# First stage of an attention, FFN and experts kernel: turned tokens, weight pieces and x's place

## The chip, the cores and the metric

One core of one Trainium2 chip. The metric is the device time of one execution in microseconds; lower is better. The engines are called TensorE (PE in rows; PEld is its weight load), VectorE (DVE), ScalarE (ACT), GpSimd (POOL) and SyncE (SP).

## The reference, cut to what matters

```python
# attention, for each of B=4 batches and H=8 heads; x: 512 x 64 tokens, state: 32 x 64 slots
scores = scale * x @ state.T                # 512 x 32
a = softmax(scores);   xread = a @ state    # softmax over the 32 slots
scores2 = scale * state @ x.T               # 32 x 512
a2 = softmax(scores2); sread = a2 @ x       # softmax over the 512 tokens
y = concat([xread, sread]), heads side by side   # 4 x 544 rows of 512
# FFN: y = g @ w_out with h = y @ w_in, g = h - tanh(h)    (512 -> 2048 -> 512)
# experts: gates from 8 normalisation rounds, sum over 8 experts of relu(y @ w1[e]) @ w2[e]
```

The FFN's weights arrive as 64-bit numbers and are taken apart in the kernel; fp32 products are made from a first part (hi, fp32r) and a second (lo) of each operand, in three matmuls (`mm3`, L92 to L95).

## The kernel before, in words

Three stages follow one another. **The first stage** is the attention of all four batches together with round 0 of the FFN. **Rounds 1 to 7** of the FFN follow (a round is 256 of the 2048 inner columns). **The expert stage** fills the rest.

In the first stage a batch b has four pairs p of heads and two groups q of two pairs. The steps, with the letters by which the order names them:

- x (`load_x`, L229): batches 0 and 1 head by head, 2 and 3 by token tile, into tiles [token, t, head, d] of their own (two buffers). A token's number is 4p + t for partition p.
- T (`tokens`, L285): four transposes turn a pair's 512 tokens into [2 x 64, 512]; t copies the result to SBUF (`keep_tokens`).
- S (`scores`, L294): two fp32 matmuls, slots as weights (128x64), the turned tokens as moving operand: scores with slots on partitions. m and 5 take the largest per row, c (`keep_scores`) copies the scores to SBUF, X is the exponential with its sum (softmax over tokens).
- O (`over_slots`, L312): four transposes of the kept scores give half of the token tiles with tokens on partitions; o, 6, E, R, 1, 2, N make the softmax over slots (o, 6, R, 1, 2 on VectorE, E on ScalarE, N on either VectorE or GpSimd).
- B (`back`, L367): four transposes of the exponentials; b copies them. G (`read`, L393): eight fp32 matmuls, the exponentials as weights (128x64), 128 columns of x moving; g (`keep_read`, L406) scales 32x64 blocks by the inverse sums (3, 4) into rows. J, Q, i (`xs_turn` and its two parts, L415 to L426) turn all rows of sread at the end.
- W, w, l: the slots' weights turned and split for the FFN's first product. M, k, r (`m_mul`, `m_hi`, `m_lo`): state times w_in, split. H, a, s, z, q: h, tanh, gate and its split (q is `h_lo` on GpSimd). Y, y: the second FFN product and its copy to the result tiles `yacc[b]`.
- F, A, I, j, C, K: the conversion of a weight piece of 128 x 256: fetch, two ScalarE steps (`words_of`), three VectorE steps (`bits_of`, L158 to L171), one GpSimd step (`number_of`), the first part by ScalarE (`hi_of`) and the second by GpSimd (`lo_of`). The first stage converts 16 pieces, for rounds 0 and 1.

`ORDER_OF_FIRST` (L737) is a list of such words, like T10 or b10V (step, batch, number, engine A, V or G). `listed` (L690) pins each word behind the last instruction of every engine, so within a word list every queue has the order of the list. What follows the list (rounds 1 to 7, and the conversion of pieces by `prep`, L198) isn't pinned: a scheduler lays it out, and it may stand between the words of the list. In the rounds `prep` runs one step of conversion per call, with fetches two pieces ahead (`AHEAD`).

`sb_turn` (L251) turns the state into block form; the state comes in through `yacc[3]`. PSUM has four banks `bank` (tag w) and four `acc_bank` (tag a); before, only the FFN's second product uses the latter in this stage.

Of the kernel before, what the change touches and what calls it, by code (L numbers as in the profile page):

```python
# [19 lines left out]
def attention_ffn_experts(  # L20
# [31 lines left out]
    AHEAD = 2  # L52
# [53 lines left out]
    if True:  # L106
# [20 lines left out]
        for j in range(NJ):  # L127
            for k in range(KD):
                pieces.append(("i", j, k, 0, w_in[k * P:(k + 1) * P, j * FC:(j + 1) * FC]))
            for f in range(2 * j, 2 * j + 2):  # L130
                for c in range(0, DM, FC):
                    pieces.append(("o", j, f, c, w_out[f * P:(f + 1) * P, c:c + FC]))

        late = pieces[2 * KD + 2:3 * KD]
        pieces[2 * KD + 2:4 * KD] = pieces[3 * KD:4 * KD] + late
        live = {}
        FIRST_PIECES = 4 * KD
        at = [FIRST_PIECES]

        def piece(step):  # L140
            return step if FIRST_PIECES <= step < len(pieces) else -1

        def fetch(n):
            if n < len(pieces) and n not in live:
                raw = mid.tile([P, FC, 2], U32, tag="raw", bufs=AHEAD + 3, name=f"raw{n}")
                nc.sync.dma_start(raw.rearrange("p n w -> p (n w)"), pieces[n][-1].bitcast(U32))
                live[n] = {"raw": raw}

        def temp(n, tag, dtype, bufs):
            live[n][tag] = mid.tile([P, FC], dtype, tag=tag, bufs=bufs, name=f"{tag}{n}")  # L150
            return live[n][tag]

        def words_of(n):
            v = live[n]
            nc.scalar.activation(temp(n, "mag", F32, 2), f32(v["raw"][:, :, 1]), AF.Abs, scale=REBASE)
            nc.scalar.mul(temp(n, "low", U32, 3), v["raw"][:, :, 0], 2.0 ** -29)

        def bits_of(n):  # L158
            v = live[n]
            t = temp(n, "bits", U32, 4)  # L160
# [16 lines left out]
        def hi_of(n):  # L177
            v = live[n]
            kind, j, r, c, _ = pieces[n]
            if kind == "i":  # L180
                hi = ffn.tile([P, FC], F32R, tag="wih", bufs=6, name=f"wih{j}_{r}")
                lo = ffn.tile([P, FC], F32R, tag="wil", bufs=6, name=f"wil{j}_{r}")
                wi_t[j, r] = hi, lo
            else:
                if r not in wo_t:
                    wo_t[r] = (
                        ffn.tile([P, DM], F32R, tag="woh", bufs=4, name=f"woh{r}"),
                        ffn.tile([P, DM], F32R, tag="wol", bufs=4, name=f"wol{r}"),
                    )
                hi, lo = (z[:, c:c + FC] for z in wo_t[r])  # L190
# [38 lines left out]
        def load_x(b, i):  # L229

            if b not in x_t:
                x_t[b] = att.tile([P, NT, H, D], F32, tag="x", bufs=2, name=f"x{b}")
            if b > 1:
                nc.sync.dma_start(x_t[b][:, i], x[b].rearrange("h (p t) d -> t p h d", t=NT)[i])
            else:
                nc.sync.dma_start(x_t[b][:, :, i], x[b, i].rearrange("(p t) d -> p t d", t=NT))
# [33 lines left out]
        sr = yacc_s  # L270
# [3 lines left out]
        class Attention:  # L274
# [3 lines left out]
            def __init__(self, b):  # L278
                self.b = b
                self.x = x_t[b].rearrange("p t h d -> p t (h d)")  # L280
                self.xt, self.sc, self.e2t, self.e1, self.ps = {}, {}, {}, {}, {}
                self.mx = att.tile([P, NQ], F32, tag="mx2", bufs=2, name=f"mx2_{b}")
                self.sm = att.tile([P, NQ], F32, tag="sm2", bufs=2, name=f"sm2_{b}")

            def tokens(self, p):  # L285
                ps = self.ps["t", p] = bank(f"xtps{self.b}_{p}")
                for t in range(NT):
                    nc.tensor.transpose(ps[:, t * P:(t + 1) * P], self.x[:, t, p * P:(p + 1) * P], ident)

            def keep_tokens(self, p, copy):  # L290
                self.xt[p] = att.tile([P, S], F32, tag="xt", bufs=4, name=f"xt{self.b}_{p}")
                copy(self.xt[p], self.ps.pop(("t", p)))

            def scores(self, q):  # L294
                b = self.b
                ps = self.ps["s", q] = bank(f"sc2ps{b}_{q}")
# [3 lines left out]

            def keep_scores(self, q):
# [1075 lines left out]
```

## Time and profile before

| | |
|---|---|
| median of 3 runs | 1775.64 us (1775.09 to 1775.74) |
| the profiled execution's own time | 1775.18 us |
| its span | 1773.4 us |
| TensorE busy | 1747.0 us, 99%, 8181 instructions |
| VectorE busy | 1201.2 us, 68% |
| ScalarE busy | 794.3 us, 45% |
| GpSimd busy | 1193.5 us, 67% |
| share of TensorE on the chain of waits | 86% |

The span runs from the first instruction to the last; the execution's own time is 1.8 us longer. Shares are of the whole span, so they say little about a stage of some 100 us: for that the busy time by stretches is to be read. A matmul's duration in a row is that of one instruction from end to end; since matmuls overlap, the time that one takes up is the distance of the starts.

### The profile page before, as it was taken

Reading aid. Unit: us, or ns where it says so; the run is one execution under the profiler, and the core shown is the slowest. Engines: PE = TensorE matmul, PEld = TensorE weight load, DVE = VectorE, ACT = ScalarE, POOL = GpSimd, SP = SyncE. Lnnn points to the kernel's source line nnn. Section 1 sums busy time; section 2 is a strip of 40 time slices with the busy share of each in tenths; the row PEclk is TensorE's granted clock in tenths of the full one; section 3 lists DMA queues with packets and bytes.
Section 4 is the critical chain, followed back from the end, with each engine's and each line's share of the span. In section 5 each row is a group of like instructions: output and inputs, shape, how many; then the busy total and the mean of one; then the engine's idle time right before and its main releaser. Section 6 shows DMA issues by size and latency. Waiting matters only on the chain.

```text
span 1773.4 us, 23139 instructions
## 1 busy us (share of the span) xinstructions
PE 1747.0 (99%) x8181; PEld 1441.1 (81%) x8181; DVE 1201.2 (68%) x1793; ACT 794.3 (45%) x1399; POOL 1193.5 (67%) x1041
## 2 busy tenths in 40 slices
PE   7999999999999999999999999999999999999998
PEld 5778888878888888888888888888888888888887
DVE  8998787556876566666666666756666666666666
ACT  7876666444333323323333323344444444444442
POOL 3575556278777677767666676567777777777774
PEclk9999999999999999999999999999999999999999
DMA  5221110017666556665556565455554655655541
GB/s 148 83 92 48 48 48 19 24 57 235 210 208 221 194 192 210 209 208 203 198 196 208 192 207 191 190 208 205 198 202 173 231 202 188 215 187 201 206 184 53
DMA packets 158759, 296.73 MB, mean 167 GB/s; under 512 B 28404, under 2 KB 107828, under 8 KB 154292
## 3 DMA queue, kind: packets, MB, share of 16 engines
q1 hardware_dynamic: 157604, 295.00, 48.3%
q8 instruction: 64, 1.05, 0.2%
q14 instruction: 51, 0.42, 0.1%
q10 hardware_dynamic: 1040, 0.26, 0.1%
HBM read 174.87 MB, written 120.36 MB: 166 GB/s over the span
## 4 chain that ended last, share of the span: by engine, by line
PE 86%; DVE 7%; ACT 3%; POOL 2%; issue 1%; DMA 1%; SPq 0%; DVEq 0%; ACTq 0%; POOLq 0%
PE p1b L1075 14%; PE p_P L1226 14%; PE p1a L1075 10%; PE p1c L1075 9%; PE p L95 7%; PE p L93 7%; PE p L94 7%; PE p1s L1127 2%; PE yps L94 2%; PE yps L93 2%; PE mP L1226 2%; PE yps L95 2%; DVE low L164 2%; PE hps L95 1%; DVE bits L168 1%
## 5 line engine op out<-in xcount | busy, mean ns | idle before, releaser
L868 POOL TENSOR_TENSOR w1l<-w1r,w1h 128x768 fp32r<-128x768 f32 (+1 forms) x96 | 170.9, 1806 | 156.9 <-ACT w1h L866 156.9
L1178 DVE SCALAR_TENSOR_TENSOR oacc<-p,pr,oacc 128x512 f32<-128x512 f32 x224 | 166.4, 745 | 111.9 <-PE p L95 111.9
L1075 PE MATMUL p1b<-xT,w1h 128*128 128x512 f32 x768 | 237.6, 390 | 0.0
L1235 DVE TENSOR_TENSOR m<-p_P,m 128x512 f32<-128x512 f32 x232 | 159.5, 689 | 86.3 <-PE p_P L1226 86.3
L93 PE MATMUL p<-w2b,hh 128*128 128x512 f32 x512 | 199.8, 390 | 1.8 <-ACT hh L1013 1.5
L94 PE MATMUL p<-w2b,hh 128*128 128x512 f32 x512 | 199.3, 389 | 0.0
L95 PE MATMUL p<-w2b,hl 128*128 128x512 f32 x512 | 197.0, 390 | 0.7 <-DVE hl L1014 0.7
L1083 DVE TENSOR_TENSOR U<-p1b,P 128x512 f32<-128x512 f32 x128 | 88.4, 691 | 150.5 <-PE p1b L1075 126.6
L1075 PEld LDWEIGHTS p1b<-xT,w1h 128*128 128x128 f32 x768 | 142.4, 188 | 28.1
L1075 PE MATMUL p1a<-xB,w1h 128*128 128x512 f32 x512 | 161.0, 395 | 0.0
L494 POOL TENSOR_TENSOR gl<-t,gh 128x512 fp32r<-128x512 f32 x64 | 86.5, 1362 | 107.9 <-ACT gh L490 106.8
L1075 PE MATMUL p1b<-xT,w1l 128*128 128x512 f32 x384 | 149.5, 389 | 0.0
L903 ACT CAST w2s<-w2r 128x1024 fp32r<-128x1024 f32 x32 | 33.7, 1052 | 231.3 <-POOL w2r L897 231.3
L1032 POOL TENSOR_TENSOR h11l<-U,h11h 128x512 fp32r<-128x512 f32 x32 | 41.4, 1295 | 126.7 <-ACT h11h L1031 67.3
L1233 ACT COPY m<-p_P 128x512 f32<-128x512 f32 x128 | 74.9, 586 | 98.2 <-PE p_P L1226 97.9
L1014 DVE SCALAR_TENSOR_TENSOR hl<-U,hh 128x512 fp32r<-128x512 f32 x64 | 99.2, 1550 | 27.8 <-ACT hh L1013 27.8
L93 PEld LDWEIGHTS p<-w2b,hh 128*128 128x128 f32 x512 | 96.1, 188 | 23.0 <-ACT hh L1013 2.6
L865 POOL TENSOR_TENSOR w1r<-w1r 128x256 f32<-128x256 f32 x128 | 94.3, 747 | 28.5 <-DMA w1r<-in_moe_w_dram 25.6
L95 PEld LDWEIGHTS p<-w2b,hl 128*128 128x128 f32 x512 | 96.0, 188 | 21.1 <-DVE hl L1014 1.3
L94 PEld LDWEIGHTS p<-w2b,hh 128*128 128x128 f32 x512 | 96.1, 188 | 19.7
L1083 DVE TENSOR_TENSOR U<-p1c,U 128x512 f32<-128x512 f32 x128 | 87.9, 686 | 33.3 <-PE p1c L1075 33.0
L1075 PEld LDWEIGHTS p1a<-xB,w1h 128*128 128x128 f32 x512 | 93.6, 188 | 17.9
(301 smaller groups left out, 4809.2 us busy)
## 6 DMA issues: line engine op xcount, KB each, us to landing
w1h<-w1h SPq DMA_DIRECT2D x64, 896.0 KB, 4.3
w1l<-w1l SPq DMA_DIRECT2D x64, 896.0 KB, 6.0
w<-w2a SPq DMA_DIRECT2D x30, 1024.0 KB, 4.8
w<-w2c SPq DMA_DIRECT2D x30, 768.0 KB, 8.2
w1r<-in_moe_w_dram SPq DMA_DIRECT2D x128, 128.0 KB, 4.4
w2r<-in_moe_w_dram SPq DMA_DIRECT2D x32, 512.0 KB, 4.0
w2a<-w2b SPq DMA_DIRECT2D x60, 256.0 KB, 3.2
w2c<-w2s SPq DMA_DIRECT2D x60, 256.0 KB, 3.8
```

Of the source, the lines that this page charges most:

```text
L93: nc.tensor.matmul(ps, whi, xhi, start=start, stop=False, **k)
L94: nc.tensor.matmul(ps, whi, xlo, start=False, stop=False, **k)
L95: nc.tensor.matmul(ps, wlo, xhi, start=False, stop=stop, **k)
L494: nc.gpsimd.tensor_tensor(out=lo, in0=h_t1.pop((j, b, i)), in1=f32(hi), op=ALU.subtract)
L865: nc.gpsimd.tensor_tensor(out=r[:, out], in0=r[:, a], in1=r[:, b], op=op)
L868: nc.gpsimd.tensor_tensor(out=lo[:, c0:c1], in0=r[:, c0:c1], in1=f32(hi[:, c0:c1]), op=ALU.subtract)
L1014: nc.vector.scalar_tensor_tensor(out=lo, in0=src, scalar=0.0, in1=f32(hi), op0=ALU.max, op1=ALU.subtract)
L1075: nc.tensor.matmul(t[z], w[:, slot, k, :], x[:, m, k, :], start=(first and k == i == 0), stop=(k == 1 and i == 2), skip_group_check=True,)
L1083: nc.vector.tensor_tensor(out=t[name], in0=a, in1=b, op=ALU.add)
L1178: nc.vector.scalar_tensor_tensor(out=o, in0=ps, scalar=w, in1=o, op0=ALU.mult, op1=ALU.add)
L1226: nc.tensor.matmul(ps, w[:, a], b, start=(i == 0 and not goes_on), stop=(i == 2 and (last or not kept)), skip_group_check=True,)
L1235: nc.vector.tensor_tensor(out=m, in0=ps, in1=m, op=ALU.add)
```

## The change

- **Tokens** are turned by plain matmuls against the identity, head by head (weights 128x64 of x, 128 moving columns), into `acc_bank`; `scores` goes there too.
- **Scores over slots** no longer come from kept scores: for each token tile and pair the turned tokens are weights (128x128) and the state's 64 columns move. `keep_scores` goes; the exponential reads the scores in PSUM. O, o, 6, E, R, 1, 2, N work by group q instead of by half.
- **The second softmax**: 3 and 4 (sums, inverses) work by q; D makes a diagonal of the inverse sums, and B multiplies the exponentials by it instead of transposing them. G has x as weights (128x64) and 32 columns of the turned exponentials as moving operand, so sread comes out turned; g and h split it batch by batch. `keep_read` and the step J, Q, i go.
- **Weight pieces** have 512 columns (two k blocks of w_in or a whole row block of w_out): 8 pieces in the first stage instead of 16; in the rounds a piece every second step, fetched one ahead. Conversion steps of the first pieces behind the list are pinned.
- **x** lies by head in the result tiles `yacc[b]`, loaded two heads at a time (16 loads instead of 24). Turned tokens of batches 0 and 1 lie in the tiles of the gate's split.
- **M**: four of eight second parts go to GpSimd, from a copy that ScalarE makes (n, rG). Shares: four of eight on VectorE (one before).
- 13 matmuls of the identity by itself stand ahead of the list, and the list is new.

The core of the diff:

```diff
-    AHEAD = 2
+    AHEAD = 1
...
+            for k in range(0, KD, 2):
+                of = w_in[k * P:(k + 2) * P, j * FC:(j + 1) * FC].rearrange("(k p) n -> p k n", p=P)
+                pieces.append(("i", j, k, of))
             for f in range(2 * j, 2 * j + 2):
+                pieces.append(("o", j, f, w_out[f * P:(f + 1) * P, :]))
...
         def piece(step):
-            return step if FIRST_PIECES <= step < len(pieces) else -1
+            n = step // 2
+            return n if step % 2 == 0 and FIRST_PIECES <= step and n < len(pieces) else -1
...
             if b not in x_t:
+                x_t[b] = yacc[b].rearrange("p k s -> p (k s)").rearrange("p (h t d) -> p h t d", h=H, t=NT)
+            nc.sync.dma_start(
+                x_t[b][:, 2 * i:2 * i + 2].rearrange("p h t d -> p h (t d)"),
+                x[b, 2 * i:2 * i + 2].rearrange("h (p t) d -> p h (t d)", t=NT),
+            )
...
             def tokens(self, p):
+                ps = self.ps["t", p] = acc_bank(f"xtps{self.b}_{p}")
                 for t in range(NT):
-                    nc.tensor.transpose(ps[:, t * P:(t + 1) * P], self.x[:, t, p * P:(p + 1) * P], ident)
+                    for r in range(2):
+                        nc.tensor.matmul(
+                            ps[D * r:D * (r + 1), t * P:(t + 1) * P], self.x[:, 2 * p + r, t, :], ident,
+                            start=True, stop=True,
+                        )
...
-                for q in range(NQ):
-                    for t in (2 * half, 2 * half + 1):
-                        o = (t % 2) * 256 + q * P
-                        nc.tensor.transpose(ps[:, o:o + P], self.sc[q][:, t * P:(t + 1) * P], ident)
+            def over_slots(self, q):
+                b = self.b
+                ps = self.ps["o", q] = bank(f"sc1ps{b}_{q}")
+                for t in range(NT):
+                    for p in (2 * q, 2 * q + 1):
+                        c = col0(b, p)
+                        nc.tensor.matmul(
+                            ps[:, t * P + c:t * P + c + 64], self.xt[p][:, t * P:(t + 1) * P],
+                            sb_raw[:, b // 2, p, c:c + 64], start=True, stop=True,
+                        )
...
+            def diagonal(self, q):
+                self.dg[q] = att.tile([P, P], F32, tag="dg", bufs=2, name=f"dg{self.b}_{q}")
+                nc.vector.tensor_scalar_mul(self.dg[q], ident, self.sm[:, q:q + 1])
...
-                    nc.tensor.transpose(ps[:, t * P:(t + 1) * P], self.sc[q][:, t * P:(t + 1) * P], ident)
+                    nc.tensor.matmul(
+                        ps[:, t * P:(t + 1) * P], self.sc[q][:, t * P:(t + 1) * P], self.dg[q], start=True, stop=True
+                    )
...
+            def read(self, _):
+                b = self.b
+                ps = self.ps["r"] = bank(f"srps{b}")
+                for p in range(NP):
+                    for t in range(NT):
+                        for r in range(2):
+                            o = t * P + col0(b, p) + NS * r
+                            nc.tensor.matmul(
+                                ps[D * r:D * (r + 1), p * NS:(p + 1) * NS], self.x[:, 2 * p + r, t, :],
+                                self.e2t[p // 2][:, o:o + NS], start=(t == 0), stop=(t == NT - 1),
+                            )
...
+        def m_keep(j, bp, q, copy):
+            m_raw[j, bp, q] = yacc_s if q else att.tile([P, 2 * FC], F32, tag="n", name=f"mraw{j}_{bp}")
+            copy(m_raw[j, bp, q], m_ps[j, bp, q])
...
-                prep()
+                listed(prep) if at[0] < PINNED else prep()
...
+        warm = acc_bank("warm")
+        for _ in range(13):
+            nc.tensor.matmul(warm[:, :P], ident, ident, start=True, stop=True)
```

The new list begins `x20 F01 x23 x22 T20 x11 x21 t20A U00 A01 F06 U10 u00 T23 u10 v10 T22` and ends, like the old one, with the last products Y of batch 3.

## Rows read from the trace of the kernel before

**Rows 1.** Busy time by stretches; columns: stretch, length, busy us (instructions) by engine, clock, DMA

```profile
0.00:40.00 40.00, 29.49 (x191) 21.65 (x191) 32.66 (x77) 29.95 (x66) 10.60 (x19) 0.96 0.59 152
40.00:104.00 64.00, 57.47 (x355) 43.43 (x355) 62.04 (x137) 53.30 (x127) 39.02 (x45) 1.00 0.29 91
104.00:385.00 281.00, 278.66 (x1330) 231.34 (x1329) 212.80 (x342) 173.66 (x364) 154.45 (x151) 1.00 0.12 38
```

**Rows 2.** TensorE's waits in 0 to 104 us, first, third and last of 16

```profile
PE xtps L288 <- DMA x<-in_x_dram: 5.8, 1, 5.8
...
PE srps L401 <- ACT e2t L374: 1.5, 1, 1.5
...
PE srps L401 <- DVE e2t L374: 0.2, 1, 0.2
```

**Rows 3.** TensorE's waits in 104 to 385 us, the two largest of three

```profile
PE ysps L95 <- DVE gsl L90: 1.2, 4, 0.3
PE yps L94 <- POOL gl L494: 0.6, 1, 0.6
```

**Rows 4.** Groups of VectorE's instructions in 0 to 104 us

```profile
L164 DVE SCALAR_TENSOR_TENSOR low<-raw,low 128x256 uint32<-128x256 uint32 x24 | 13.4, 565 | 0.3 <-ACT low L156 0.3
L450 DVE TENSOR_TENSOR ml<-mps,mh 64x512 fp32r<-64x512 f32 x16 | 11.0, 686 | 0.2
...
L413 DVE TENSOR_SCALAR yacc_s<-srps,sm 32x64 f32<-32x64 f32 x20 | 5.6, 281 | 0.3
...
L349 DVE TENSOR_SCALAR m<-m 128x16 f32<-128x16 f32 x8 | 2.2, 295 | 0.0
```

**Rows 5.** Groups of TensorE's instructions in 0 to 104 us

```profile
L288 PE MATMUL xtps<-ident,x 128*128 128x128 f32 x64 | 11.4, 329 | 6.2 <-DMA x<-in_x_dram 5.8 <-DVE mx L306 0.4
...
L401 PE MATMUL srps<-x,e2t 128*64 128x128 f32 x128 | 9.4, 281 | 1.6 <-ACT e2t L374 1.5 <-DVE e2t L374 0.2
```

**Rows 6.** TensorE in order of time, 51 to 54 us; columns: start, us, engine, line, operation

```profile
51.42 1.09 PE L401 MATMUL srps<-x,e2t 128*64 128x128 f32 x16
52.44 1.09 PE L288 MATMUL xtps<-ident,x 128*128 128x128 f32 x8
53.29 0.47 PE L93 MATMUL yps<-gh,woh 128*128 128x512 f32 x1
```

**Rows 7.** One line's instructions: shortest, median and longest in ns (L401, L656, L667)

```profile
L401 PE MATMUL srps<-x,e2t x128: 272/273/413, 18.6 to 69.4; 128*64 128x128 f32 x128
...
L656 PE MATMUL ltps<-add,lt x16: 251/251/272, 379.1 to 384.6; 16*128 16x8 f32 x16
...
L667 PE MATMUL lps<-x2s_raw,wg x8: 275/275/377, 392.6 to 393.5; 128*128 128x128 f32 x8
```

**Rows 8.** TensorE in order of time at 379 and at 392 us

```profile
379.08 1.05 PE L656 MATMUL ltps<-add,lt 16*128 16x8 f32 x8
...
392.62 1.16 PE L667 MATMUL lps<-x2s_raw,wg 128*128 128x128 f32 x8
```

**Rows 9.** Loads in 0 to 110 us: count, KB each, median us to landing

```profile
x<-in_x_dram SPq DMA_DIRECT2D x8, 256.0 KB, 3.7
```

**Rows 10.** TensorE in order of time, 5 to 11 and 34 to 37 us

```profile
5.81 1.09 PE L288 MATMUL xtps<-ident,x 128*128 128x128 f32 x4 [5.81 <-DMA x<-in_x_dram]
...
10.99 2.25 PE L299 MATMUL sc2ps<-xt,sb_raw 128*64 128x512 f32 x8
...
34.83 1.97 PE L288 MATMUL xtps<-ident,x 128*128 128x128 f32 x8
36.45 0.78 PE L93 MATMUL hps<-ath,mh 128*128 128x512 f32 x1
```

**Rows 11.** Busy time by stretches, 35 to 36 us (the clock is third from the end)

```profile
35.00:36.00 1.00, 1.00 (x6) 1.00 (x7) 0.96 (x3) 0.49 (x1) 0.00 (x0) 0.50 0.00 0
```

**Rows 12.** Groups of GpSimd's instructions in 0 to 104 us

```profile
L175 POOL TENSOR_TENSOR bits<-bits,low 128x256 uint32<-128x256 uint32 x22 | 16.8, 761 | 34.0 <-DVE bits L168 23.9 <-DVE sm L365 8.4 <-DVE low L164 1.2
L494 POOL TENSOR_TENSOR gl<-t,gh 128x512 fp32r<-128x512 f32 x8 | 10.7, 1342 | 3.2 <-ACT gh L490 3.2
```

More of the change, by code (lines that the diff above doesn't have):

```diff
@@ L269, in attention_ffn_experts @@
         at_t = {}
-        sr = yacc_s
         xs_hi = ffn.tile([P, KD, P], F32R, name="xs_hi")
@@ L326, in less_largest @@
                 v, m = self.ps.pop(("o", half))
-                e = att.tile(list(v.shape), F32, tag="e1", bufs=2, name=f"e1_{self.b}_{half}")
+                e = att.tile(list(v.shape), F32, tag="e1", bufs=4, name=f"e1_{self.b}_{half}")
                 nc.vector.tensor_tensor(
@@ L391, in weights_lo @@
                 nc.vector.tensor_tensor(out=lo, in0=self.ps.pop(("w", q)), in1=f32(hi), op=ALU.subtract)
-            def read(self, q):
+            def read(self, _):
                 b = self.b
-                ps = self.ps["r", q] = bank(f"srps{b}_{q}")
-                for t in range(NT):
-                    for g in range(2):
-                        u = 4 * q + 2 * ((g + b) % 2)
-                        nc.tensor.matmul(
-                            ps[64 * g:64 * (g + 1), :2 * D], self.e2t[q][:, t * P + 64 * g:t * P + 64 * (g + 1)],
-                            self.x[:, t, u * D:(u + 2) * D], start=(t == 0), stop=(t == NT - 1),
-                        )
@@ L415, in xs_turn @@
-        def xs_turn():
-            ps = h_ps["xs"] = bank("xsps")
-            for k in range(KD):
-                nc.tensor.transpose(ps[:, k * P:(k + 1) * P], sr[:, k * P:(k + 1) * P], ident)
-        def xs_hi_of():
-            nc.scalar.copy(xs_hi, h_ps["xs"].rearrange("a (k c) -> a k c", k=KD))
-        def xs_lo_of():
-            nc.vector.tensor_tensor(
-                out=xs_lo, in0=h_ps.pop("xs").rearrange("a (k c) -> a k c", k=KD), in1=f32(xs_hi), op=ALU.subtract
-            )
+                ps = self.ps["r"] = bank(f"srps{b}")
@@ L429, in m_mul, with read_lo @@
+            def read_lo(self, _):
+                hi, lo = (z[:, :, NS * self.b:NS * (self.b + 1)] for z in (xs_hi, xs_lo))
+                ps = self.ps.pop("r")[:, :KD * NS].rearrange("a (k s) -> a k s", k=KD)
+                nc.vector.tensor_tensor(out=lo, in0=ps, in1=f32(hi), op=ALU.subtract)
         def m_mul(j, bp, q):
@@ L446, in m_hi, with m_lo_kept @@
                 nc.scalar.copy(hi, v)
+        m_raw = {}
+        def m_keep(j, bp, q, copy):
+            m_raw[j, bp, q] = yacc_s if q else att.tile([P, 2 * FC], F32, tag="n", name=f"mraw{j}_{bp}")
+            copy(m_raw[j, bp, q], m_ps[j, bp, q])
+        def m_lo_kept(j, bp, q):
+            m_ps[j, bp, q] = m_raw.pop((j, bp, q))
+            for v, hi, lo in m_parts(j, bp, q):
+                nc.gpsimd.tensor_tensor(out=lo, in0=v, in1=f32(hi), op=ALU.subtract)
+            del m_ps[j, bp, q]
         def m_lo(j, bp, q):
@@ L723, in attention_ffn_experts @@
             PARTS[z] = lambda b, n, fn=fn: fn(b)
-        for z, fn in zip("Mkr", (m_mul, m_hi, m_lo)):
+        for z, copy in COPY.items():
+            PARTS["n" + z] = lambda b, n, copy=copy: m_keep(b // 2, b % 2, n, copy)
+        for z, fn in (("M", m_mul), ("k", m_hi), ("rV", m_lo), ("rG", m_lo_kept)):
             PARTS[z] = lambda b, n, fn=fn: fn(b // 2, b % 2, n)
```

136 lines of the change are left out of this document (59 added, 77 removed), and 4 rows, old and new, of the table PARTS.

## The prediction

> **What bounds the kernel now.** I read the busy time by stretches first, then TensorE's waits, then the instructions in order of time. The stretches show the parts [rows 1]: in 0 to 104 us, the first stage, VectorE is busy 94.7 us of 104 (32.66 + 62.04), and TensorE's row has holes; from 104 to 385 us TensorE is busy 278.66 us of 281, and behind that no less. So the span is TensorE's work plus its holes, and nearly all holes lie in the first stage. The waits give them [rows 2]: 5.8 us until the first piece of x, then 15 short waits of 0.2 to 1.5 us with 11.0 us in sum, most released by VectorE or ScalarE. From 104 to 385 us the waits are 1.8 us in the two largest groups [rows 3]. What VectorE does in the first stage is mostly small: the weight conversions, the second parts of M, the 32x64 scalings of the second read, and steps of 16 columns [rows 4].
>
> So VectorE holds TensorE up by some 11 us and not more; a change that relieves VectorE can earn those 11 us, and pays for each microsecond of matmul that it adds.
>
> **Prices on TensorE.** A plain fp32 matmul stands in the trace as two instructions, a transpose as one: the reads are 64 matmuls and x128, the turned tokens 64 transposes and x64 [rows 5]. Both kinds stand beside each other at full clock [rows 6]: 16 read instructions (weights 128x64, 128 moving columns) take 1.02 us from start to the next start, and within the block, whose last instruction takes 0.273 us from end to end [rows 7], (1.09 - 0.273) / 15 = 0.0545 us each; 8 transposes take 0.85 us, 0.106 each. With weights of 128 columns a short matmul is dearer [rows 7, 8]: eight with 8 moving columns take 1.05 us, (1.05 - 0.251) / 7 = 0.114 each, and eight with 128 moving columns (1.16 - 0.275) / 7 = 0.126. Eight columns cost as much as 128, so what limits them is the load, not the stream.
>
> **The change on TensorE, part by part.**
> Turned tokens (L288): 16 blocks of 4 transposes, 0.425 us each, become 16 blocks of 8 matmuls against the identity, 16 instructions of exactly the read's shape: 1.02 us. +9.5 us.
> Scores over slots (L317): 8 blocks of 4 transposes (0.42 us) become 8 blocks of 8 matmuls, 16 instructions with 128x128 weights and 64 moving columns. Nearest is 0.114: 1.82 us a block, +11.2 us. If the load hid wholly, 0.0545: +3.6.
> Turning back with the diagonal (L370): 4 transposes become 4 matmuls, 8 instructions of 128x128 by 128. At 0.126 that is 1.01 us against 0.42, eight times: +4.7 us. At 0.0545: +0.1.
> Second read (L401): 2 blocks of 1.02 us per batch become one of 32 matmuls, 64 instructions with 128x64 weights and 32 moving columns. No row has this shape. If only moving columns counted, a quarter of 0.0545, it would be 0.9 us a batch, -4.7 us in all; at the price of a 128-column load, 0.114, 7.3 us, +21. Weights of 64 columns stand at 0.0545, and moving columns hardly mattered where the load was the longer, so I take 0.0545: 3.5 us a batch, +5.8 us.
> The Trainium skill's page TensorE: Matmul & The Clock Gate, section LDWEIGHTS, states that a weight load takes its columns divided by 1.2 in ns, whatever the number of rows; its section on the 56 ns gap gives about 25 ns as the least distance of two short matmuls. By the first the read would be 53 ns an instruction, its term +5.5 us and the sum below +30.5, by the second 25 ns, -1.8 and +23.2, estimates from that page; no row here has 64-column weights with few moving columns, so the trace doesn't decide between them.
> The turn of the slots' rows (L418) goes: four transposes, -0.4 us.
> Sum: 9.5 + 11.2 + 4.7 + 5.8 - 0.4 = **+30.8 us** of TensorE work; low ends together +8.1, high ends +46.
>
> **What it takes back.** The first block of tokens needed four loads of x, issued one after the other from 0.74 us on; now it needs the first alone. A load of 256 KB, the new size, takes 3.7 us to landing [rows 9]; with 0.7 us for its issue (an estimate) TensorE starts near 4.4 instead of 5.81: -1.4 us.
> The first 24 transposes (4, 8 and 12) took 5.18 us, from 5.81 to 10.99, where 24 x 0.106 is 2.5, so they ran at half pace; from 34.83 us 8 transposes took 1.62 us instead of 0.85 [rows 10], with the granted clock at 0.50, the level of 1.2 GHz, after TensorE had waited for e2t [rows 2, 11]. Together 3.4 us. The 13 dummy matmuls (26 instructions) need nothing but the identity, so they run while x is on its way and cost nothing themselves; if they raise the clock, they take back up to 2.6 us. I take 2.5 of the 3.4.
> Of the 11.0 us of waits I take 8 back and leave 3, between none and all, for VectorE's relief.
>
> VectorE: the scalings in L413 go (5.6 us), half of the second parts of M (8 x 0.69 = 5.5) go to GpSimd; three more shares on VectorE cost perhaps 1 us each (estimate, above the 0.69 of another 512-column step), the diagonals and the sums by half perhaps 4 (estimate: some 20 instructions, most shorter than the 0.295 us of a 16-column step); weight pieces of 512 columns halve the count of three conversions, worth between nothing (if they cost by column) and half (if by instruction), which is 6.7 us for the largest of them; I take 3 for the three [rows 4]. Net some 7 us off 94.7, in a stage that becomes longer: VectorE is under 85% busy there and no longer the bound. GpSimd takes 8 halves of M at about 1.34, the price of its 512-column split [rows 12]: +10.7 against 49.6 busy [rows 1]; hidden under TensorE. ScalarE loses the eight copies of the scores and gains four of M. The first conversions for the round after the stage, which now stand in it as well (x24 where the stage needs 16), are pinned behind it, one more relief of VectorE. SP loses 8 loads of x and 8 of weights. x lying in the result tiles adds a wait of the first copy of y of each batch on its last read; in the order of the parts that read comes well before, so it costs nothing; were it late, ScalarE's later copies and the banks of y would queue behind it.
>
> From 104 us on nothing changes but the wide pieces, under a TensorE that is full there [rows 1]: 0. The expert stage is untouched.
>
> **The forecast.** 30.8 - 1.4 - 2.5 - 8 = +18.9 us. The profiled execution took 1775.18 us with a span of 1773.4; the median of the runs shown is 1775.64, so it stands for them. 1775.2 + 18.9 = **1794.1 us**. Its own range is 1780 (over slots, diagonal and read together 10 us cheaper, all waits and all of the clock back) to 1805 (of the three, only the earlier start comes back).
>
> **The rivals.**
> *Faster: the loads hide.* If short fp32 matmuls run as fast as their moving columns let them, TensorE's addition is near 8 us, less than the 1.4 + 3.4 + 11.0 = 15.8 us that can come back: 8 - 15.8 is -8, some 1767 us. It decides at an addition of 15.8. For it: VectorE is the fuller engine in the first stage now [rows 1]. Against it: eight moving columns at 0.114 [rows 8]. 13%.
> *No change.* The addition is 13 to 19 us, because over slots, diagonal and read run at half to two thirds of the prices I took, and all 15.8 us come back: 1772 to 1779. 10%.
> *Much slower: the clock falls.* The new over-slots and read blocks, 8 x 1.82 + 4 x 3.5 = 29 us, stream few columns a load; if half of that ran at 1.2 GHz, 14 us come on top: 1808. For it: the clock did fall once, at 35 us, after TensorE had stood still for 1.5 us [rows 2, 11]. The Trainium skill, same page, Part 1, says that "the default state is throttled, and activity releases the throttle"; this trace shows one such fall and no stretch of loads with 32 columns each. 8%.
> *Wide pieces late.* GpSimd's single instruction grows from 0.76 to about 1.34 us [rows 12] and stands ahead of gl, for which TensorE waits 0.6 us now [rows 3]; with 1 us in each of seven rounds +7, 1801. Inside the forecast's range.
>
> **How the numbers follow.** 0.2% of this kernel, about what a measurement can tell from no change, is 3.6 us. Faster 13%; same 10%; slower 77%, of which 69% is the forecast with the late pieces and 8% the clock. The range for 8 in 10 leaves out the faster case below and half of the clock case above, with a little of the case of no change: 1773 to 1808.
>
> **What would show it.** Right: in the first stage the tokens' x256 near 0.055 us from one to the next, over slots x128 near 0.11, the diagonal x64 near 0.12, the read x256 near 0.055; TensorE's row full from about 5 us on, VectorE's with gaps, the step to the even part (seen at 104 us now) near 120 us, and the expert stage as long as before. Wrong: over slots or the read well below these prices; or TensorE's holes as large as before, which would mean that another wait took VectorE's place; or a longer second part, which would point to the wide pieces.

## The result and the profile after

The changed kernel takes **1800.37 us** (median of four runs, 1800.2 to 1801.66), the one before, run beside it, 1775.55 (four runs): a ratio of **1.0142**, 95% interval 1.0124 to 1.0159. Slower, by 24.8 us where 18.9 were forecast. The profiled execution took 1800.44 us, its span is 1798.6, 25.2 more than before.

Busy time of the changed kernel by stretches, columns as in [rows 1]:

```profile
0.00:40.00 40.00, 32.77 (x312) 28.58 (x314) 26.37 (x49) 24.37 (x46) 16.99 (x19) 0.91 0.58 191
40.00:104.00 64.00, 64.00 (x655) 54.43 (x650) 45.72 (x105) 39.57 (x79) 28.94 (x23) 1.00 0.13 43
...
150.00:160.00 10.00, 6.74 (x37) 5.30 (x35) 9.19 (x12) 6.58 (x12) 7.23 (x6) 1.00 0.34 122
160.00:170.00 10.00, 6.71 (x26) 5.31 (x26) 9.82 (x15) 8.15 (x15) 6.88 (x5) 0.83 0.46 159
170.00:180.00 10.00, 5.80 (x19) 4.46 (x20) 9.89 (x13) 5.31 (x10) 8.58 (x6) 0.83 0.18 61
```

VectorE's first stage is lighter than forecast: 72.1 us busy of the first 104 instead of 94.7. Up to the first turn of the gated rows (`tsps`, at 116.5 us instead of 99.2) it is 78.5 us instead of 89.9, so 11.4 less where some 7 were forecast. TensorE is full from 40 to 150 us. But there is a hole before 40 us, and three lean stretches at 150 to 180 us, in round 1 and at its end, where VectorE is as full as it had been in the first stage.

TensorE's waits of the changed kernel, in 0 to 130 us (two rows, that is all there are) and in 130 to 411 us (the first three and the fifth of six); columns: line, releaser, sum in us, times, longest:

```profile
PE atps L398 <- DVE e L367: 5.6, 1, 5.6
PE warm L774 <- POOL ident masks.py:199: 1.5, 1, 1.5
...
PE hps L93 <- DVE gsl L90: 3.4, 1, 3.4
PE hps L95 <- DVE ml L467: 3.2, 1, 3.2
PE mps L93 <- DVE ml L467: 3.1, 1, 3.1
...
PE yps L94 <- POOL gl L511: 0.6, 1, 0.6
```

The fifteen short waits of [rows 2] have become one of 5.6 us. Three waits of over 3 us stand where [rows 3] showed nothing above 1.2.

TensorE's groups in 0 to 130 us, to be set beside [rows 5]:

```profile
L290 PE MATMUL xtps<-ident,yacc 128*64 128x128 f32 x256 | 16.7, 284 | 0.0
...
L323 PE MATMUL sc1ps<-sb_raw,xt 128*128 128x64 f32 x128 | 15.6, 276 | 0.0
...
L386 PE MATMUL e2ps<-dg,sc 128*128 128x128 f32 x64 | 9.5, 298 | 0.1
...
L419 PE MATMUL srps<-e2t,yacc 128*64 128x32 f32 x256 | 8.2, 223 | 0.0
```

What an instruction takes up is read in order of time, from start to next start. TensorE of the changed kernel at the start, around 27 us and from 40 to 48 us:

```profile
1.46 5.33 PE L774 MATMUL warm<-ident 128*128 128x128 f32 x26 [1.46 <-POOL ident masks.py:199]
6.72 1.09 PE L290 MATMUL xtps<-ident,yacc 128*64 128x128 f32 x16
7.75 1.09 PE L256 MATMUL sbps<-ident,yacc 128*128 128x128 f32 x8
8.77 3.71 PE L290 MATMUL xtps<-ident,yacc 128*64 128x128 f32 x64
...
27.07 1.09 PE L398 MATMUL atps<-ident,e 128*128 128x128 f32 x4 [5.63 <-DVE e L367]
28.29 2.05 PE L386 MATMUL e2ps<-dg,sc 128*128 128x128 f32 x8
29.99 0.56 PE L93 MATMUL mps<-wih,sb_hi 128*128 128x256 f32 x1
...
40.59 1.16 PE L386 MATMUL e2ps<-dg,sc 128*128 128x128 f32 x8
41.51 0.36 PE L93 MATMUL mps<-wih,sb_hi 128*128 128x256 f32 x1
...
42.30 1.89 PE L323 MATMUL sc1ps<-sb_raw,xt 128*128 128x64 f32 x16
44.13 1.09 PE L290 MATMUL xtps<-ident,yacc 128*64 128x128 f32 x16
45.05 1.03 PE L308 MATMUL sc2ps<-xt,sb_raw 128*64 128x512 f32 x4
45.91 2.01 PE L419 MATMUL srps<-e2t,yacc 128*64 128x32 f32 x64
47.75 1.06 PE L308 MATMUL sc2ps<-xt,sb_raw 128*64 128x512 f32 x4
```

A block of tokens takes 1.03 us (6.72 to 7.75), 0.0545 an instruction as forecast; a block over slots 1.83 (42.30 to 44.13), 0.114; the diagonal 0.92, 0.115. The read surprises: 64 instructions in 1.84 us, **0.029 each**, where I took 0.0545. And the dummies take 5.26 us, 0.2 each, so the first tokens start at 6.72 us, 0.9 later than in [rows 10].

These prices are means. How single instructions start is seen when the window is ended a little later each time. The read, in windows that end at 45.92, 45.95 and 46.01 us:

```profile
45.91 0.20 PE L419 MATMUL srps<-e2t,yacc 128*64 128x32 f32 x2
45.91 0.26 PE L419 MATMUL srps<-e2t,yacc 128*64 128x32 f32 x4
45.91 0.32 PE L419 MATMUL srps<-e2t,yacc 128*64 128x32 f32 x6
```

They start in pairs. The loop alternates between the two halves of the output's partitions, and an instruction for one half starts together with its neighbour for the other; the next pair follows 0.058 us later. So 0.029 is half the distance of two pairs. The tokens start in pairs too, 0.109 us apart with 128 moving columns, and so did the read before [rows 6]: their 0.0545 is half of that. Over slots, where each weight has all 128 columns, there are no pairs: one instruction starts every 0.112 us.

**The ledger.** I split both runs at two events: the second turn of a round's gated rows (`tsps`), at 111.07 us before and 125.02 after, and the one two rounds later, at 193.72 and 217.88. In each stretch an instruction is given the distance to the next start, less the wait that the profile names there:

| us | before | after | difference |
|---|---|---|---|
| turned tokens | 10.2 | 15.8 | +5.6 |
| over slots | 4.5 | 14.9 | +10.4 |
| turning back, diagonal | 4.2 | 8.1 | +3.9 |
| second read | 8.7 | 7.7 | -1.0 |
| turn of the slots' rows | 0.8 | 0 | -0.8 |
| dummies | 0 | 5.3 | +5.3 |
| all other matmuls | 66.1 | 66.2 | +0.1 |
| before the first instruction | 5.8 | 1.5 | -4.3 |
| waits | 10.8 | 5.6 | -5.2 |
| **to the first event** | 111.1 | 125.0 | **+14.0** |
| next two rounds, waits | 0.3 | 10.7 | +10.5 |
| next two rounds, work | 82.4 | 82.1 | -0.3 |
| **rest of the span** | 1579.7 | 1580.7 | **+1.0** |

The tokens are up by less than 9.5, in good part because 24 of the turns before had run at half pace [rows 10]. "All other" holds 17 FFN matmuls more by the first event (114 of the second product against 97), some 3.9 us of work that the next rounds no longer have. At equal work the first stage has lost 10.1 us (14.0 - 3.9), and the two rounds behind it 14.1 (10.2 + 3.9): 10.5 in waits, the other 3.6 in slower matmuls behind these: the granted clock is 0.83 in 160 to 180 us, and 0.96 in the mean of the two rounds where it was 1.00 before.

### The profile page after: what moved, and what is told of

It is laid out like the page before. It is cut to its first block, busy times and chain, and to the rows that moved or that the text cites. A ratio compares the mean times of both kernels' runs of the same rounds, so it can differ in the third digit from the quotient of the medians.

```text
span 1798.6 us, 23656 instructions
## 1 busy us (share of the span) xinstructions
PE 1770.9 (98%) x8651; PEld 1471.2 (82%) x8651; DVE 1175.7 (65%) x1689; ACT 784.8 (44%) x1292; POOL 1193.8 (66%) x982
## 4 chain that ended last, share of the span: by engine, by line
PE 91%; POOL 3%; DVE 3%; DMA 2%; issue 1%; ACT 1%; SPq 0%; DVEq 0%; POOLq 0%; ACTq 0%
PE p1b L1092 14%; PE p_P L1243 14%; PE p1a L1092 9%; PE p1c L1092 9%; PE p L95 7%; PE p L93 7%; PE p L94 7%; PE yps L94 3%; PE yps L95 3%; PE yps L93 3%; PE p1s L1144 2%; PE mP L1243 2%; PE hps L93 2%; PE hps L94 2%; PE hps L95 2%; DMA w2r<-in_moe_w_dram 1%
```

## The experiments

My theory after the result: (1) the two rounds pay for conversions that the pin moved out of the first stage; (2) a short matmul pays by the columns of its weights; (3) work of TensorE ahead of the hole at 21 to 27 us costs nothing, work behind it counts fully. The rivals: wide pieces are dear wherever they stand; a short matmul has a fixed price, or alternating halves make it cheap; work counts everywhere. The first kernels change the changed kernel in one point each.

**The pin.**

```diff
-        PINNED = 6 * KD
+        PINNED = 0
```

> The changed kernel with the first conversions behind the list not pinned (one constant to 0), all else as changed. In the changed kernel TensorE waits 11.5 us in 130 to 411 us (2.0 before), 10.7 of them between 154 and 171 us, while VectorE and GpSimd convert pieces one after the other. Theory A (the pin moved these conversions out of the first stage, where VectorE now has room, and round 1 has to do them in a burst): the waits of the rounds fall to 2 to 4 us and the time by 7 to 11 us, to 1789 to 1793. Rival B (the wide pieces are late whatever their place): the waits stay at 8 us or more and the time within 2 us of 1800.4.

Measured: 1792.49 us (1791.92 and 1793.06), 7.9 less than the changed kernel. TensorE's waits of this kernel in 0 to 411 us, the first, second and fourth:

```profile
PE atps L398 <- DVE e L367: 8.7, 2, 5.6
PE ltps L692 <- DVE pr L693: 1.6, 1, 1.6
...
PE yps L94 <- POOL gl L511: 1.3, 2, 0.7
```

All three waits of the rounds are gone; the two rounds take 78.1 us (131.55 to 209.68) instead of 92.9. The first stage pays part of it: its event comes at 131.55 instead of 125.02, with a second wait for shares of 3.0 us. VectorE's three steps of conversion (L164, L167, L171) show the move: in the changed kernel 24 of them stand ahead of the first event (15.1 us busy) and 45 in the two rounds behind it (41.3 us), here 43 (31.7 us) and 26 (25.4 us). The pieces are as wide as in the changed kernel, so width is not what made the rounds late: place is.

**Turned tokens by transposes again**, with x still in the result tiles, but by token and head, so that one transpose turns two heads.

```diff
-                x_t[b] = yacc[b].rearrange("p k s -> p (k s)").rearrange("p (h t d) -> p h t d", h=H, t=NT)
+                x_t[b] = yacc[b].rearrange("p k s -> p (k s)").rearrange("p (t h d) -> p t h d", h=H, t=NT)
...
+                    both = self.x[:, t].rearrange("a h d -> a (h d)")[:, p * P:(p + 1) * P]
+                    nc.tensor.transpose(ps[:, t * P:(t + 1) * P], both, ident)
```

> The changed kernel with x by token and head in the result tiles (32 loads of one head each), so that a pair's 128 columns are adjacent and tokens are turned by 64 transposes, as in the kernel before, instead of 256 matmul instructions. Work theory (the first stage is bound by TensorE, and each microsecond of its work is one of the span): 16 blocks of 1.0 us become 0.43, so 8.7 to 9.5 us less, 1791 to 1792. Rival (the holes and the chain through VectorE and ScalarE set the end of the stage): 3 us or less, 1797 or more. If x's loads in short pieces are what the stage then waits for, TensorE's waits on DMA show it.

Measured: 1799.16 us (1798.08 and 1800.23), only 1.2 less, though 16 blocks are each some 0.6 shorter. The first shares' turn starts at 28.44 us, 1.4 later than in the changed kernel, behind a wait of 7.5 us instead of 5.6. From there to the first turn of the gated rows it is 84.4 us instead of 89.5: the nine blocks behind the hole give 5.1, in full, the seven ahead of it nothing. These seven aren't a clean test, since x's loads have changed with them: TensorE waits 1.2 us for loads and 0.7 for ScalarE between 8 and 12 us, where the changed kernel doesn't wait. The 3.7 us that are left are all there at the gates (416.9 us, 421.0 in the changed kernel); of this run's span they make 2.3. So the hole decides, as the rival of the forecast had it, and why less than 3.7 reaches the end stays open.

**Over slots in halves**: each matmul as two, with weights of 64 columns.

```diff
+                        for r in (0, 64):
                             nc.tensor.matmul(
-                                ps[:, t * P + c:t * P + c + 64], self.xt[p][:, t * P:(t + 1) * P],
+                                ps[r:r + 64, t * P + c:t * P + c + 64], self.xt[p][:, t * P + r:t * P + r + 64],
```

> The changed kernel with each matmul of the scores over slots cut into two with weights of 64 columns instead of 128, into the upper and lower half of the partitions: 256 instructions instead of 128. Load theory 1 (a short fp32 matmul costs its weights' columns, 64 at half the price of 128): no change, 0.055 each instead of 0.115, the block stays at 1.8 us, 1799 to 1801. Theory 2 (the 0.029 of the second read, whose matmuls alternate between the halves, holds for every matmul with 64-column weights and few moving columns): the block falls to about 1 us, 7 us less, 1793. Theory 3 (what costs is the instruction with 128 output rows, not the load): between the two.

Measured: 1793.87 us (1793.5 and 1794.23), 6.5 less, with twice the instructions. TensorE in order of time, two blocks over slots:

```profile
13.09 2.03 PE L324 MATMUL sc1ps<-sb_raw,xt 128*64 128x64 f32 x64
14.95 1.03 PE L308 MATMUL sc2ps<-xt,sb_raw 128*64 128x512 f32 x4
```

64 instructions in 1.86 us, 0.029 each, against 0.114 for one with weights of 128 columns and the same 64 moving. A fixed price per instruction would have doubled the block; it halved. The two halves go to different partitions of the output, and they start in pairs like the read's, 0.058 us apart. Two of the eight blocks lie ahead of the hole and are 1.9 us shorter together; the shares' turn starts at 26.10 us, 1.0 earlier, behind a wait of 6.7. So work ahead of the hole isn't free where the shares hang on it: about half of it counted here.

**The read half by half**, so that neighbours write the same half of PSUM's partitions.

```diff
-                    for t in range(NT):
-                        for r in range(2):
+                    for r in range(2):
+                        for t in range(NT):
```

> The changed kernel with the loops of the second read exchanged: four matmuls into one half of the partitions, then four into the other, instead of alternating. In the changed kernel its instructions lie 0.029 us apart, where 0.0545 was forecast. Theory 1 (alternation lets the load of one half run under the matmul of the other): the distance rises to about 0.055, the four blocks from 1.85 to 3.5 us, 6.6 us more, 1807. Theory 2 (the distance is that of short instructions with 64-column weights, alternating or not): 0.029 stays, 1800 to 1801.

Measured: 1802.23 us (1801.17 and 1803.29), 1.9 more, in two runs of which one lies among the changed kernel's four: no clear change. The 64 instructions start within 46.01 and 48.26 us, some 0.035 each. The first of them, in windows that end at 46.05 and at 46.16 us:

```profile
46.01 0.25 PE L419 MATMUL srps<-e2t,yacc 128*64 128x32 f32 x2
46.01 0.37 PE L419 MATMUL srps<-e2t,yacc 128*64 128x32 f32 x4
```

While only one half has work they start singly, one every 0.058 us. By 46.28 us there are seven: the other half has begun beside the rest of the first. So exchanging the loops only delays the side-by-side; it doesn't take it away, and the run can't tell alternation from no alternation. What it shows is the price within one half, 0.058; the 0.029 of the read is two halves at once.

**The turned tokens alone**, in the kernel before.

```diff
-                    nc.tensor.transpose(ps[:, t * P:(t + 1) * P], self.x[:, t, p * P:(p + 1) * P], ident)
+                    for r in range(2):
+                        o = p * P + D * r
+                        nc.tensor.matmul(
+                            ps[D * r:D * (r + 1), t * P:(t + 1) * P], self.x[:, t, o:o + D], ident,
```

> The kernel before with one part of the change alone: tokens turned by plain matmuls (256 instructions) instead of transposes (64), x and all else where they were. It adds 16 x 0.57 = 9.1 us of TensorE work to a first stage in which TensorE has 17 us of holes. Work theory in its plain form (every microsecond of work is one of the span): 1784 to 1785. Hole theory (work placed ahead of a wait that VectorE ends is swallowed by it): 2 to 5 us more, 1777 to 1780.

Measured: 1779.86 us (eight runs) against 1776.06 before (eleven): ratio 1.0019 (1.0008 to 1.0031). So 3.8 of some 9 us show, the number of the hole theory. The trace doesn't show its mechanism: in the profiled execution (1781.35 us), by the ledger, the turned tokens are up by 7.8 us and all work by 7.0, the waits fall by 1.0 and the first block starts 0.8 earlier (5.03), so 5.2 are left at the first event (116.27). Little is swallowed there, and what makes 3.8 of it in the median stays open.

**Five dummies instead of thirteen.**

```diff
-        for _ in range(13):
+        for _ in range(5):
```

> The changed kernel with 5 dummy matmuls instead of 13. The 26 instructions take 5.3 us (0.2 us each, the half-pace price of a 128x128 load) and end at 6.7 us, while the first load of x should be there near 4. Theory 1 (the dummies' tail delays the first tokens): these start at 4 to 5 us; what TensorE wins is swallowed by the wait for the shares at 21 to 27 us, so the time moves by less than 1.5 us. Theory 2 (the early start moves the whole chain up): 2 us less, 1798. Theory 3 (the clock stays low for want of dummies): the first 80 token instructions take 0.1 us instead of 0.055 and the wait at 27 us comes later by 1 us or more.

Measured: 1800.13 us (1798.71 and 1801.55): no change. TensorE at the start:

```profile
1.46 2.50 PE L774 MATMUL warm<-ident 128*128 128x128 f32 x10 [1.46 <-POOL ident masks.py:199]
4.45 1.61 PE L290 MATMUL xtps<-ident,yacc 128*64 128x128 f32 x16 [0.49 <-DMA yacc<-in_x_dram]
7.10 1.06 PE L256 MATMUL sbps<-ident,yacc 128*128 128x128 f32 x8 [1.04 <-DVE yacc L249]
```

The first tokens start at 4.45, the forecast's 4.4, 2.3 us earlier. Ten of their 16 instructions run at half pace, so the first block takes 1.61 from first start to last end, instead of 1.09; then TensorE waits 1.0 us for the state. Of the 2.3 us 0.7 are left at the state's turn (7.10 instead of 7.75) and at the shares' turn (26.39 instead of 27.07). The wait before it is 5.6 us as with 13 dummies: the hole doesn't swallow the 0.7, it comes earlier with the chain that ends it. The two runs, 2.8 us apart, don't show what becomes of them.

**Three blocks of tokens moved into the hole.**

```diff
-F05 R20 W21 n01A
+F05 R20 T13 T01 T10 W21 n01A
...
-T13 321 l21 k00 r01G W20 421 t13V T01 T10 w20
+321 l21 k00 r01G W20 421 t13V w20
```

> The changed kernel with three words of the list moved ahead of W21, the word at which TensorE waits 5.6 us for the shares: T13, T01 and T10, three blocks of turned tokens that need no more than x and a bank. Hole theory: they run in the hole, 2 to 3 us less, and another 1 to 2 us because the clock need not fall (it falls at 27 us after the wait): 1795 to 1798. Rival (banks: the second or third of them waits for the exponential of the scores, and W21 with them): no change or up to 2 us more.

Measured: 1798.72 us (1798.69 and 1798.75), 1.7 less. The 48 instructions run from 21.36 us, for 3.0 us, the wait shrinks from 5.6 to 2.6, and the shares' turn stays at 26.99. That is the theory's mechanism; 2.8 of the 3 us arrive at the first turn of the gated rows (113.71 against 116.54), 1.7 at the end. The other part of the forecast, 1 to 2 us from the clock, didn't come: in 28 to 31 us it is 0.50 here too, after a wait of 2.6 us, and the diagonal takes 1.73 us (28.20 to 29.93), 1.70 without the move.

**Four changes together**: unpinned, halves, tokens in the hole, five dummies.

> The changed kernel with four of these together: conversions not pinned, scores over slots with 64-column weights, T13, T01 and T10 ahead of W21, 5 dummies. If the parts add up (-8.0 and -6.5 measured, -2 to -5 and 0 to -2 expected): 1779 to 1784, still slower than the kernel before, since the turned tokens and the diagonal stay dearer. If the unpinned conversions take the room that the shorter stage had, the two measured gains overlap: 1786 or more.

Measured: 1784.25 us (four runs, 1783.07 to 1784.93), 16.1 less than the changed kernel. The single ones add up: 7.9 + 6.5 + 1.7 + 0.2 = 16.3. Against the kernel before 1.0048 (1.0028 to 1.0067).

**Transposes on top of these four.**

> The four changes together (1784.25 us) and, fifth, tokens turned by transposes from x by token in the result tiles. It takes 16 x 0.57 = 9.1 us of TensorE work away; seven of the blocks lie ahead of the wait for the shares at 20 to 27 us, nine behind it, and T13, T01 and T10 of those nine now run in its hole. Work behind the wait counts, work ahead of it doesn't: 6 x 0.57 = 3.4 us less, 1781. If all 16 count, 1775; if x's loads in short pieces hold the first blocks up as in the run with transposes alone (the wait for the shares ended 1.4 us later), 1782 to 1784.

Measured: 1782.42 us (four runs, 1781.19 to 1785.93), 1.0040 of before (1.0025 to 1.0054). In the median 1.8 less than with four, with ranges that overlap, though 16 blocks are some 0.6 shorter each: the shares' turn stands at 26.41, because the moved tokens, ahead of it, now wait 4.9 us themselves.

**GpSimd out of the way of the shares.** A second part of M on GpSimd goes behind the shares.

```diff
-R21 x02 I06 X20 x31 r11G C00 x00
+R21 x02 I06 X20 x31 C00 x00
...
-N20V j06 w21
+N20V r11G j06 w21
```

> The five changes together with one word moved: the two second parts of M on GpSimd (r11G), which run at 21.9 to 25.0 us, go behind the shares N20V. Between 20 and 27 us VectorE's steps stretch while GpSimd works (a 16-column step takes 1.23 us instead of 0.17 at its best, the shares 1.53 instead of 1.07, the bits 1.49 instead of 0.42). Theory (VectorE is held up by GpSimd's work beside it): W21 starts 1.5 to 2.5 us earlier, at 24.5 to 25.5 us, and the time falls by 1 to 2 us against the run beside it. Rival (the chain of dependences alone sets W21): no change.

In this kernel the copy of the next M overwrites the one that the moved step reads: one group's second part of M is made from another's copy, so its time is only a hint, and its rows are read for the order of the steps. Measured: 1781.62 us (five runs, 1780.79 to 1786.66), no change. VectorE of the kernel with five changes, and then of this one, around the first shares:

```profile
21.70 1.49 DVE L171 TENSOR_SCALAR bits<-mag 128x512 uint32<-128x512 uint32 x1
23.11 1.23 DVE L355 TENSOR_SCALAR m<-m 128x16 f32<-128x16 f32 x1
...
24.66 1.42 DVE L363 TENSOR_TENSOR e<-e,m 128x512 f32<-128x512 f32 x1
```

```profile
20.34 0.42 DVE L171 TENSOR_SCALAR bits<-mag 128x512 uint32<-128x512 uint32 x1
20.67 0.16 DVE L355 TENSOR_SCALAR m<-m 128x16 f32<-128x16 f32 x1
...
21.35 0.69 DVE L363 TENSOR_TENSOR e<-e,m 128x512 f32<-128x512 f32 x1
```

The same three steps shrink from 4.14 us to 1.27, and the shares are done at 22.04 instead of 26.08. But the shares' turn starts at 26.13 all the same: the moved tokens stand ahead of it in the queue and waited 4.8 us, now for ScalarE.

**Five dummies in the kernel before.**

```diff
+        warm = acc_bank("warm")
+        for _ in range(5):
+            nc.tensor.matmul(warm[:, :P], ident, ident, start=True, stop=True)
```

> The kernel before with five dummy matmuls of the identity ahead of its list, nothing else. They run while the first pieces of x are on their way (1.5 to 4 us). Theory (TensorE's first 24 transposes, at half pace, delay the start of VectorE's long chain): the state's turn (8 transposes, 1.7 us at half pace) ends 0.5 to 1 us earlier and so does all that follows: 1774.5 to 1775, just faster. Rival (VectorE's chain starts by x's landing): no change, 1775.6. If the clock doesn't rise before the tokens arrive: no change either, and the transposes stay at 0.21 us each.

Measured: 1776.02 us (eleven runs) against 1775.8 (twenty): ratio 1.0001 (0.9992 to 1.0010). Nothing. The tokens start at 6.17 for want of x, the state's turn takes 1.71 us (7.05 to 8.76), where it takes 1.02 in the changed kernel (7.75 to 8.77), and of the eight transposes from 8.76 us three still run at half pace.

**The shares first**: the five changes without the moved tokens, with both steps of M (`r11G`, `n01A`) behind the shares.

> The five changes without the three token blocks ahead of W21, and with r11G and the raw copy n01A that follows it behind the shares N20V (the raw copy shares a buffer with r11G's operand, so both move). In the run with r11G alone moved, the shares took 0.69 us instead of 1.42 and the first were done at 22.0 us, but W21 came at 26.1 because the token blocks ahead of it waited for a bank until 24.4. Theory (the hole before W21 is VectorE held up by GpSimd, plus, with the blocks moved, a bank): W21 starts at 22 to 23 us, TensorE waits there 1 to 2 us, and the time falls by 2 to 4 us against the five changes (1782.42), to 1778 to 1780, still above the kernel before. Rival (later waits of the first stage give it back): 1781 or more.

Measured: 1781.41 us (five runs, 1779.32 to 1782.76), 1.0035 of before (1.0021 to 1.0049), 1.0 less than with five changes, with ranges that overlap. That is the rival's number. TensorE where the hole was, and at the longest wait that is left:

```profile
22.36 0.63 PE L394 MATMUL atps<-ident,e 128*128 128x128 f32 x4 [3.00 <-DVE e L363]
...
75.97 1.12 PE L394 MATMUL atps<-ident,e 128*128 128x128 f32 x4 [4.18 <-DVE e L363]
```

The first shares come 4 us sooner, as meant; at most one is left in the median, and a later share makes TensorE wait 4.2 us, which may have eaten up the rest. In that trace VectorE has ten steps of conversions in 64 to 75 us, four of them stretched to between 1.04 and 1.78 us beside GpSimd's, and the share behind them takes 1.74 (0.69 at 21.52 us). This is the best version of the changed kernel, 5.7 us behind the kernel before in the median. Its profiled execution, by the ledger: +8.5 us to the first event (119.57), -4.8 in the two rounds, -1.9 to the gates (398.5 against 396.7), and +2.3 in the expert stage, where TensorE's longest wait for ScalarE is 2.0 us instead of 0.8. I didn't try to clear the second place, and why the untouched stage waits longer stays open.

## Why the prediction was right, and where not

Slower, inside the range, 6 us beyond the forecast; errors of both signs lie in the sum. Two of the prediction's own signs of being wrong came: the read well below its price, and a longer second part.

- **What bounds the kernel**: right. VectorE held TensorE by some 11 us and no more, and the added matmuls were paid for.
- **Prices.** Tokens 0.0545, over slots 0.114, diagonal 0.115 against 0.126: the last two terms are off by 0.8 us each. **The second read is the term that failed**: forecast +5.8, measured -1.0. "Weights of 64 columns stand at 0.0545, and moving columns hardly mattered" took half of a pair's 0.109 us for the price of one instruction, and carried over from weights of 128 columns that moving columns hardly count. With weights of 64 columns they do: a pair takes 0.109 us with 128 moving columns and 0.058 with 64 or 32, which the halved scores over slots show a second time. With weights of 128 columns one instruction takes 0.112 to 0.126 whether 8, 64 or 128 move. Of the two rules of the Trainium skill (TensorE: Matmul & The Clock Gate) that the prediction weighed, the first agrees with the trace: by the section LDWEIGHTS a load of 64 columns would be 53 ns, an estimate, and 58 lie between two starts in one half. The least distance of about 25 ns in its section on the 56 ns gap is near the mean of 29, but that mean is two halves side by side, so it isn't what the read shows. What the sum lacked is that the halves run at once.
- **The dummies "cost nothing themselves"**: wrong, +5.3 us of work. They stand ahead of the tokens in TensorE's queue, and at half pace 26 of them reach beyond the arrival of x. The forecast start of 4.4 us is that of the run with five. The first blocks did run at full pace behind them, but the hole took 2.4 us back: the granted clock in 28 to 33 us is 0.50, and three blocks there took 5.1 us (28.29 to 33.42) where the same three take 2.7 later.
- **Waits**: -8 forecast, -5.2 measured. The rest is one wait for the first shares, which the change had put on VectorE, behind a conversion and beside GpSimd; in the last run, with the two steps of M moved from there, it was 3.0 us instead of 5.6.
- **"From 104 us on nothing changes but the wide pieces"**: the largest error, +10.5 us of waits. The prediction named the pin, and booked it as "one more relief of VectorE"; it didn't ask where the conversions go. They went into round 1, where they come on top of that round's own. The unpinned kernel has them in the first stage again, pays 6.5 us there (131.55 against 125.02) and saves 14.7 in the two rounds. The rival "wide pieces late" had put +7 on GpSimd's `gl`, spread over seven rounds: that wait is 0.6 us as before, and the place, the engine and the cause were others.
- **The rivals.** The loads hide nowhere: the read, with 32 moving columns, goes no faster than the halved scores over slots with 64. Over slots at 0.114 was what kept the faster case away. The clock did fall, but behind a wait and not in the blocks of short matmuls, which ran at full pace.

- **Tokens and clock**: +9.5 and -2.5 forecast; by the ledger +5.6, and the matmuls that the change doesn't touch another -3.8 at equal count. The FFN's `h` alone takes 0.234 us an instruction where it took 0.263, 72 times: the kernel before had lost more than the 3.4 us that I had seen, in pace or in waits that no row names.

So the sum came out near because errors cancel: 14.0 us cheaper (read 6.8, tokens and clock 5.2, over slots, diagonal and slots' turn 2.0), 20.3 dearer (start 2.4, waits 2.8, everything behind the first stage 15.1).

## What to carry to other kernels

Price a short fp32 matmul by the columns of its weights, see whether two of them run side by side before a mean is carried over, and cut one of 128 columns in two, one for each half of the output's partitions, when 64 columns or fewer move. When a change moves background work out of a stage, book it where it arrives, with what stands there already, and not only as relief where it leaves. A saving on the bounding engine counts in full behind that engine's long wait for another (5.1 us of nine blocks of tokens); ahead of it, only as far as the chain that ends the wait starts earlier (1.0 of 1.9 us over slots), so shorten that chain first.

## What was not expected of the hardware

Two matmuls with half the weights, one for each half of the output's partitions, run side by side: a pair every 0.058 us, where one with all 128 columns takes 0.114, with the same 64 columns moving. With 128 moving columns a pair takes 0.109, and a split would win next to nothing. Columns of the weights and rows of the output go together in all these shapes, so no run tells which of them sets the price.

VectorE's conversion steps, scalings and shares, which read and write SBUF, can stretch beside GpSimd, by a wait and not by a share; its reductions don't, and neither do steps that read PSUM (0.68 us beside GpSimd as elsewhere). VectorE and GpSimd of the changed kernel, around the hole:

```profile
22.43 1.49 DVE L171 TENSOR_SCALAR bits<-mag 128x512 uint32<-128x512 uint32 x1
23.84 1.23 DVE L359 TENSOR_SCALAR m<-m 128x16 f32<-128x16 f32 x1
...
25.39 1.53 DVE L367 TENSOR_TENSOR e<-e,m 128x512 f32<-128x512 f32 x1
26.85 0.67 DVE L355 TENSOR_REDUCE m<-e 128x16 f32<-128x512 f32 x1
```

```profile
21.90 3.14 POOL L462 TENSOR_TENSOR ml<-yacc_s,mh 64x512 fp32r<-64x512 f32 x2 [0.27 <-ACT mh L451]
25.12 1.26 POOL L198 TENSOR_TENSOR wil<-bits,wih 128x512 fp32r<-128x512 f32 x1
26.34 1.72 POOL L178 TENSOR_TENSOR bits<-bits,low 128x512 uint32<-128x512 uint32 x1
```

GpSimd's two steps from 21.90 end at 23.63 and at 25.04, the next at 26.38. VectorE's `bits`, 0.42 us where nothing runs beside it, ends at 23.92, and the step of 16 columns, 0.17 at best, at 25.07: each ends just after one of GpSimd's. The share (0.69 alone) ends at 26.92, 0.5 us after the next of GpSimd's. The reduction from 26.85 is not stretched. The Trainium skill, SBUF — State Buffer, section SBUF: two separate sides, has this as an exclusive lock held for a whole instruction, for VectorE's two-port modes and for steps with two SBUF operands; these rows agree, as far as GpSimd's spans are exact. The three stretched steps make 3.0 us of the wait of 5.6 (1.07, 1.06 and 0.84). In the two rounds the 45 steps of conversion take 41.3 us, where at their shortest (0.41, 0.68 and 0.41) they would take 22.2; no run took GpSimd's steps away there, so their part in the burst isn't shown.

At the start the column of the granted clock is no guide: in the kernel before with dummies the state's turn took 1.71 us, where 1.02 is full pace, in a stretch whose row says 1.00:

```profile
7.05 1.92 PE L254 MATMUL sbps<-ident,yacc 128*128 128x128 f32 x8
```

```profile
7.00:11.00 4.00, 3.63 (x22) 3.30 (x20) 1.71 (x3) 2.69 (x6) 0.00 (x0) 1.00 0.96 260
```
